# x + alpha * fx, streamed through one core: the stores on a queue of their own, with a small store of zeros ahead of them

## The chip, the cores and the metric

The kernel runs on one core of a Trainium2 chip. The metric is device time in microseconds, and lower is better. Three runs of the kernel before took 151.98 to 152.3 us, with a median of 152.07 us.

## The reference

The inputs are `x` and `fx`, both bfloat16 of 512 x 32 x 640, and one bfloat16 number `alpha`. The output has the shape and type of `x`.

```python
def reference(x, fx, alpha):
    return x + alpha * fx
```

Every element is read once from each of two arrays of 20.97 MB and written once to a third. That makes 62.92 MB through the DMA engines, and a multiply and an add for each element.

## The kernel before

The three arrays are seen as 128 partitions by 81920 elements, cut into 80 columns of K = 1024 elements (2 KB in each partition, 256 KB in all). A partition's whole row is contiguous in memory. `X` cuts `x` and the output into three pieces of 32, 32 and 16 columns. `FX` cuts `fx` into five of 16, 16, 19, 16 and 13. So the cuts of the two arrays are different, and a piece of `x` is finished by more than one piece of `fx`. `X_CUTS` loads the first 4 columns of piece 0 of `x` with a transfer of their own.

There are two buffers for pieces of `x` (pool `wide`) and two for pieces of `fx` (pool `fs`). The sum is made in place, in the buffer of `x`, and the store goes out of that buffer. A third piece of `x` must therefore wait until the store of the first has landed, and a third piece of `fx` until VectorE has used the first.

The order is written out by hand. `PLAN` is a list of steps that are emitted one after the other, and each engine and queue keeps that order for its own instructions:

- `x i` is `load_x` (L77): a load of piece i of `x`, issued on the sync queue (SP).
- `f j` is `load_f` (L85): a load of piece j of `fx`, issued on the sync queue.
- `c j i` is `compute` (L92): one VectorE instruction, `x_piece = fx_piece * alpha + x_piece`, over the columns that pieces j and i have in common.
- `s i` is `store` (L104): a store of piece i, issued on the sync queue.
- `a` is `alpha_to_lanes` (L111 to L117): alpha is loaded, and a matmul with a row of ones brings it to all 128 partitions.

```python
PLAN = "x 0, a, f 0, f 1, x 1, c 0 0, f 2, c 1 0, s 0, f 3, x 2, c 2 1, f 4, c 3 1, c 3 2, s 1, c 4 2, s 2"
```

(In the kernel there is one step on each line.) An instruction at the head of the sync queue that waits for a semaphore holds up all that stands behind it. With all loads and stores on that queue, the transfers also run in the order of the plan. ScalarE has no work in this kernel, and GpSimd (Pool) has four small memsets that the framework puts at the start.

`done` collects the instructions that a final no-op of the sync queue (`rest`, L126) waits for, all but the last store. After it comes the end of the program, which waits for everything.

Of the kernel before, what the change touches and what calls it, by code (L numbers as in the profile page):

```python
# [2 lines left out]

# [4 lines left out]

ACT = mybir.ActivationFunctionType
ALU = mybir.AluOpType  # L10
F32 = mybir.dt.float32
BF16 = mybir.dt.bfloat16

K = 1024
P = 128


X = [(0, 32), (32, 64), (64, 80)]
FX = [(0, 16), (16, 32), (32, 51), (51, 67), (67, 80)]

X_CUTS = {0: (4,)}
PLAN = """
x 0
a
f 0
f 1
x 1
c 0 0
f 2
c 1 0  # L30
s 0
f 3
x 2
c 2 1
f 4
c 3 1
c 3 2
s 1
c 4 2
s 2  # L40
"""


@with_exitstack
def kernel(
    ctx: ExitStack,
    tc: tile.TileContext,
    x: bass.AP,
    fx: bass.AP,
    alpha: bass.AP,  # L50
    out: bass.AP,
):

    nc = tc.nc
    xv = x.flatten_outer_dims().rearrange("(p n) d -> p (n d)", p=P)
    fxv = fx.flatten_outer_dims().rearrange("(p n) d -> p (n d)", p=P)  # L60
    ov = out.flatten_outer_dims().rearrange("(p n) d -> p (n d)", p=P)
    assert xv.shape[1] == X[-1][1] * K == FX[-1][1] * K

    consts = ctx.enter_context(tc.tile_pool(name="consts", bufs=1))
    psum = ctx.enter_context(tc.tile_pool(name="psum", bufs=1, space=bass.MemoryType.PSUM))
    wide = ctx.enter_context(tc.tile_pool(name="wide", bufs=2))
    fs = ctx.enter_context(tc.tile_pool(name="fs", bufs=2))
    ctx.enter_context(tc.manual_schedule())

    xt, ft = {}, {}  # L70
    done = []

    def load_x(i):
        a, b = X[i]
        xt[i] = wide.tile([P, max(e - s for s, e in X) * K], x.dtype, tag="x", name="x_t")
        for c, d in pairwise((a, *X_CUTS.get(i, ()), b)):
            r = nc.sync.dma_start(  # L77
                out=xt[i][:, (c - a) * K : (d - a) * K], in_=xv[:, c * K : d * K]
            )
            done.append(r)  # L80

    def load_f(j):
        a, b = FX[j]
        ft[j] = fs.tile([P, max(e - s for s, e in FX) * K], fx.dtype, tag="f", name="f_t")
        r = nc.sync.dma_start(out=ft[j][:, : (b - a) * K], in_=fxv[:, a * K : b * K])  # L85
        done.append(r)

    def compute(j, i):
        (fa, fb), (xa, xb) = FX[j], X[i]
        a, b = max(fa, xa), min(fb, xb)  # L90
        piece = xt[i][:, (a - xa) * K : (b - xa) * K]
        r = nc.vector.scalar_tensor_tensor(  # L92
            out=piece,
            in0=ft[j][:, (a - fa) * K : (b - fa) * K],
            scalar=lanes["a_f"][:],
            in1=piece,
            op0=ALU.mult,
            op1=ALU.add,
        )
        done.append(r)  # L100

    def store(i):
        a, b = X[i]
        r = nc.sync.dma_start(out=ov[:, a * K : b * K], in_=xt[i][:, : (b - a) * K])  # L104
        done.append(r)

    lanes = {}

    def alpha_to_lanes():
        a_1 = consts.tile([1, 1], alpha.dtype, name="a_1")  # L110
        done.append(nc.sync.dma_start(out=a_1[:], in_=alpha[None, :]))  # L111
        ones = consts.tile([1, P], alpha.dtype, name="ones")
        nc.vector.memset(ones[:], 1.0)  # L113
        a_ps = psum.tile([P, 1], F32, name="a_ps")
        done.append(nc.tensor.matmul(a_ps[:], ones[:], a_1[:], start=True, stop=True))  # L115
        lanes["a_f"] = consts.tile([P, 1], F32, name="a_f")
        nc.vector.tensor_copy(out=lanes["a_f"][:], in_=a_ps[:])  # L117

    does = {"x": load_x, "f": load_f, "c": compute, "s": store, "a": alpha_to_lanes}
    for step in PLAN.split("\n"):  # L120
        if step:
            what, *of = step.split()
            does[what](*map(int, of))


    rest = nc.sync.nop(nofuse=True)  # L126
    info = mybir.DependencyInfo(mybir.DependencyClass.Sync, mybir.DependencyReason.DATA)
    for i in done[:-1]:
        tc.add_manual_dep(rest.ins, i.ins.name, info, reason="all but the last store")


# [1 line left out]
_INS = ['x', 'fx', 'alpha']  # L133
_OUTS = [((512, 32, 640), 'bfloat16')]


# [23 lines left out]
```

## Time and profile before

| | us |
|---|---|
| median of three runs | 152.07 |
| span of the profiled execution | 150.2 |
| VectorE (DVE) busy | 86.8 |
| of that, the six steps of L92 | 86.5 |
| VectorE idle ahead of L92, waiting for a load of fx | 25.5 |
| sync queue waiting at L104 for VectorE | 56.2 |
| sync queue at L77 waiting for a store to land | 25.7 |

The profile gives no separate total for the profiled execution beside its span, so its span is compared with the median of the runs: that is 1.9 us above. In the profile, `SPq` is the sync queue as an issuer of transfers; "us to landing" is the time from the issue of a transfer to the arrival of its last part. A line of the timeline gives the start, the duration, the engine, the line of the kernel and the operation, and in square brackets how long the engine had been idle and what released it. DMA shares are means over the 16 DMA engines.

### The profile page before, as it was taken

How to read it: one execution, taken by the hardware profiler on the slowest of the kernel's cores; microseconds unless marked ns; L12 is line 12 of the kernel's file. 1: busy time of each engine (PE TensorE's matmuls, PEld its weight loads, DVE VectorE, ACT ScalarE, POOL GpSimd, SP SyncE). 2: the span in 40 equal slices, each digit the busy share in tenths (PEclk: the TensorE clock that was granted, in tenths of full speed). 3: DMA queues.
4: the chain of work that ended last, by engine and by line, in shares of the span. 5: the costliest groups of instructions: out<-in, count | busy, mean ns of one | idle time of the engine just before them, and what ended most of it. 6: DMA issues, size and time to landing. Idle time of an engine off the chain costs nothing.

```text
span 150.2 us, 78 instructions
## 1 busy us (share of the span) xinstructions
PE 0.2 (0%) x1; PEld 0.1 (0%) x1; DVE 86.8 (58%) x8; POOL 0.2 (0%) x4
## 2 busy tenths in 40 slices
PE   0000000000000000000000000000000000000000
PEld 0000000000000000000000000000000000000000
DVE  0000000049999999970399999106999999980000
POOL 0000000000000000000000000000000000000000
DMA  5997989999969696999696999999999969696994
GB/s 179 589 428 305 489 384 419 436 454 471 576 297 559 279 559 279 497 394 435 279 559 279 559 401 410 445 419 419 419 393 454 620 279 559 279 559 297 454 463 183
DMA packets 1730, 62.92 MB, mean 419 GB/s; under 512 B 194, under 2 KB 194, under 8 KB 194
## 3 DMA queue, kind: packets, MB, share of 16 engines
q1 hardware_dynamic: 1730, 62.92, 98.1%
HBM read 41.94 MB, written 20.97 MB: 419 GB/s over the span
## 4 chain that ended last, share of the span: by engine, by line
DMA 54%; DVE 35%; SPq 1%; issue 0%; DVEq 0%
DMA f_t<-in_fx_dram 54%; DVE x_t L92 35%; SPq L77 1%; SPq L111 0%; DVEq L92 0%
## 5 line engine op out<-in xcount | busy, mean ns | idle before, releaser
L92 DVE SCALAR_TENSOR_TENSOR x_t<-f_t,a_f,x_t 128x16384 bf16<-128x16384 bf16 (+3 forms) x6 | 86.5, 14438 | 25.5 <-DMA f_t<-in_fx_dram 25.5
L117 DVE COPY a_f<-a_ps 128x1 f32<-128x1 f32 x1 | 0.2, 159 | 21.5 <-PE a_ps L115 21.5
L113 DVE MEMSET ones<- 1x128 bf16 x1 | 0.2, 165 | 0.8 <-PEq L144 0.8
L115 PE MATMUL a_ps<-a,ones 1*128 1x1 bf16 x1 | 0.2, 158 | 22.2 <-DMA a<-in_alpha_dram 22.2
L144 POOL MEMSET const-bfloat16-1.0<- 128x1 bf16 x1 | 0.1, 103 | 0.0
L144 POOL MEMSET const-uint8-127<- 128x1 uint8 x1 | 0.1, 103 | 0.0
L115 PEld LDWEIGHTS <-ones 1*128 1x128 bf16 x1 | 0.1, 100 | 1.0 <-DVE ones L113 1.0
L144 POOL MEMSET const-float32-1.0<- 128x1 f32 x1 | 0.1, 100 | 0.0
L144 POOL MEMSET const-float32-0.0<- 128x1 f32 x1 | 0.1, 99 | 0.2 <-issue 0.2
## 6 DMA issues: line engine op xcount, KB each, us to landing
f_t<-in_fx_dram SPq DMA_DIRECT2D x3, 4096.0 KB, 35.6
x_t<-in_x_dram SPq DMA_DIRECT2D x1, 7168.0 KB, 21.3
f_t<-in_fx_dram SPq DMA_DIRECT2D x1, 4864.0 KB, 24.1
x_t<-in_x_dram SPq DMA_DIRECT2D x1, 4096.0 KB, 19.2
out_dram<-x_t SPq DMA_DIRECT2D x1, 4096.0 KB, 14.9
f_t<-in_fx_dram SPq DMA_DIRECT2D x1, 3328.0 KB
x_t<-in_x_dram SPq DMA_DIRECT2D x1, 1024.0 KB, 4.8
out_dram<-x_t SPq DMA_DIRECT2D x2, 24.7
```

The source lines that it names most:

```text
L77: r = nc.sync.dma_start(out=xt[i][:, (c - a) * K : (d - a) * K], in_=xv[:, c * K : d * K])
L92: r = nc.vector.scalar_tensor_tensor(out=piece, in0=ft[j][:, (a - fa) * K : (b - fa) * K], scalar=lanes["a_f"][:], in1=piece, op0=ALU.mult ...
L113: nc.vector.memset(ones[:], 1.0)
L115: done.append(nc.tensor.matmul(a_ps[:], ones[:], a_1[:], start=True, stop=True))
L117: nc.vector.tensor_copy(out=lanes["a_f"][:], in_=a_ps[:])
L144: nc = _bacc.Bacc("TRN2", target_bir_lowering=False, num_devices=1)
```

## The change

A tile of 128 x 256 zeros, `blank`, is made by a memset on GpSimd and stored to the first 256 elements of every row of the output. That store is issued on ScalarE's queue, as the first instruction of the kernel there. The later store of piece 0 writes the same places with the result, and it waits until the store of zeros has landed. All three stores of results are issued on ScalarE's queue too, in the same order. The sync queue keeps the loads of `x`, `fx` and alpha.

```diff
+HEAD = 256
 X_CUTS = {0: (4,)}
@@
     ctx.enter_context(tc.manual_schedule())
+    done = []
+
+    blank = consts.tile([P, HEAD], out.dtype, name="blank")
+    nc.gpsimd.memset(blank[:], 0.0)
+    done.append(nc.scalar.dma_start(out=ov[:, :HEAD], in_=blank[:]))
 
     xt, ft = {}, {}
-    done = []
@@
     def store(i):
         a, b = X[i]
-        r = nc.sync.dma_start(out=ov[:, a * K : b * K], in_=xt[i][:, : (b - a) * K])
+        r = nc.scalar.dma_start(out=ov[:, a * K : b * K], in_=xt[i][:, : (b - a) * K])
         done.append(r)
```

## The prediction

> **What bounds the kernel now.** I read the engine shares, then the DMA part, then the chain and the waits of the sync queue, and last the order of time around the three stores.
>
> ```profile
> span 150.2 us, 78 instructions
> PE 0.2 (0%) x1; PEld 0.1 (0%) x1; DVE 86.8 (58%) x8; POOL 0.2 (0%) x4
> DMA packets 1730, 62.92 MB, mean 419 GB/s; under 512 B 194, under 2 KB 194, under 8 KB 194
> q1 hardware_dynamic: 1730, 62.92, 98.1%
> ```
>
> VectorE is busy for 58%, the 16 DMA engines for 98.1%, all on one queue. 1730 less 194 small packets is 1536, or twelve transfers of 128: each partition row of a transfer is one packet, and each of the 16 engines carries 8 rows of every transfer. So the bound is bytes through the DMA engines, and the chain (54% DMA, 35% VectorE) only follows who released whom beside a full queue.
>
> ```profile
> out_dram<-x_t SPq DMA_DIRECT2D x1, 4096.0 KB, 14.9
> ...
> x_t<-in_x_dram SPq DMA_DIRECT2D x1, 1024.0 KB, 4.8
> ...
> x_t<-in_x_dram SPq DMA_DIRECT2D x1, 58.3
> ```
> ```profile
> 2.90 0.45 SPq L77 DMA_DIRECT2D x_t<-in_x_dram  x1
> ...
> 49.59 0.33 SPq L85 DMA_DIRECT2D f_t<-in_fx_dram  x1
> 66.78 0.35 SPq L104 DMA_DIRECT2D out_dram<-x_t  x1
> 67.19 0.42 SPq L85 DMA_DIRECT2D f_t<-in_fx_dram  x1
> 73.80 20.48 DVE L92 SCALAR_TENSOR_TENSOR x_t<-f_t,a_f,x_t 128x19456 bf16<-128x19456 bf16 x1 [7.04 <-DMA f_t<-in_fx_dram]
> 93.37 0.33 SPq L77 DMA_DIRECT2D x_t<-in_x_dram  x1
> 94.31 0.33 SPq L85 DMA_DIRECT2D f_t<-in_fx_dram  x1
> 102.84 17.41 DVE L92 SCALAR_TENSOR_TENSOR x_t<-f_t,a_f,x_t 128x13312 bf16<-128x13312 bf16 x2 [8.55 <-DMA f_t<-in_fx_dram]
> 116.95 17.96 SPq L104 DMA_DIRECT2D out_dram<-x_t  x2
> 120.46 14.08 DVE L92 SCALAR_TENSOR_TENSOR x_t<-f_t,a_f,x_t 128x13312 bf16<-128x13312 bf16 x1 [0.21 <-DMA f_t<-in_fx_dram]
> ```
>
> From these the landings: x 1 at 2.90 + 58.3 = 61.2; f 2 at 73.7 (VectorE starts on it); store 0 at 93.4 (x 2, which takes its buffer, is issued); f 3 at 102.8; f 4 at 120.4; the last store (the second in the merged line at 116.95, issued at 116.95 + 17.96 - 0.34 = 134.6, with 14.9 to landing) at 149.5; 0.7 of ending follows. Store 0 moves 32 columns of 1024 in 93.4 - 73.7 = 19.7; x 2 and f 4 move 29 in 17.6. That is 0.605 us a column for loads and stores alike. Two places stand out. f 2 has 19 columns, 11.5 us, and took 12.5: **1.0 us is lost**, just while the first store stands behind it in the queue. The second store, issued at 116.95 behind f 4, cost nothing: f 4 still landed on time. At the head, x 0's first 1 MB needs 2.4 us of data and lands 4.8 after issue. The busy times by window show no DMA (last two columns) until 1.7:
>
> ```profile
> 0.00:1.70 1.70, 0.00 (x0) 0.10 (x1) 0.17 (x1) 0.20 (x4) 1.00 0.00 0
> 1.70:5.50 3.80, 0.00 (x0) 0.00 (x0) 0.00 (x0) 0.00 (x0) 1.00 1.34 517
> ```
>
> So of the 4.8, about 1.0 is from issue (0.73) to first packet, 2.4 is data, and some 1.4 is a slow start.
>
> **The change part by part.** The sum is made against the span of 150.2; the median of 152.07 is 1.9 above it, and I keep that 1.9.
>
> *Issues.* Three store issues of 0.35 us leave the sync queue and four come to ScalarE's queue, which holds nothing else. In the compiled order f 3 now waits for VectorE's second step itself (it takes f 1's buffer), so it goes out at about 66.8 instead of 67.2. x 2 still waits for store 0 to land, f 4 for VectorE's third step behind it; stores 1 and 2 wait on ScalarE for their VectorE steps, with nothing queued behind them but each other. The DMA queue was full throughout: worth 0. The cover is f 2's or f 3's data still moving; if that runs out, an issue shows its 1.0.
>
> The Trainium skill (DMA: Bandwidth & Descriptors, "Issuing engines are not separate DMA queues") says that issuing from more engines saves only the sequencer's issue time. By that rule alone the sum would be 152.07 plus the blank's bytes, 152.2; the trace agrees about the issues but shows the 1.0 us at the first store, which the rule has no word for.
>
> *The blank store.* A Pool memset of 128x256 lies between 0.1 (Pool's 128x1 row) and perhaps 0.5 us, and only ScalarE's queue waits for it. 64 KB is a quarter of a column, 0.15 us of data. It has no row of its own: from 0.15, up to 1.2 if the first-store loss simply comes along to the head. Below 0.15 nothing can take it, as the bytes do move.
>
> *The loss at the first store.* It belongs to the first write only (the second had none). Between -1.0 (gone) and 0 (paid at the head instead). The blank's rows reach the engines at about 2.1 (Pool 0.75 to 1.0, issue, 1.0 latency), in the 1.4 us of slow start, so I take that most of it is covered: 0.3 paid. With the bytes: -1.0 + 0.3 + 0.15 = -0.55.
>
> *Sharing between the queues.* Before, a store waited its turn behind the loads. Now it shares each engine with them. No row of before has two queues, so this has bounds only. I take turns by packet, since a packet is a row here: a 64 KB row of store 0 (2.42 us) against a row of f 2 (1.44) or f 3 (1.21). At 67.8 f 2 has two or three rows left per engine; each waits for a store row, so f 2 lands at about 78 to 80. VectorE's third step (20.5) ends at 98.5 to 101. Store 0 lands at about 97.5, with three or four f 3 rows (3.6 us or more) left to hide x 2's 1.0. f 3 lands at 102 either way, as the bytes are the same. VectorE starts on f 3 there, store 1 goes out 14.1 later at 116.2, first packet 117.2; f 4 has two rows left (undisturbed it would land at 119.5), which wait for one or two store rows: 122.0 to 124.4. VectorE's last step ends at 136.1 to 138.5, store 2's first packet is at 137.1 to 139.5, and store 1 ends at 138.8. So a hole of **0 to 0.9 us** before the last store; half a microsecond of later start on ScalarE's queue, or a load row going first, closes it. I take 0, the end that two things lead to, and keep 0.9 in the range.
>
> The Trainium skill (same page, "Queues, rings and completion order") states that an engine goes round its queues and switches at packet boundaries. No row of before can confirm it. Were all 8 rows of a transfer one turn, store 0 would follow f 2 as before, and the sum would also be -0.55.
>
> Sum: 150.2 - 0.55 = 149.65 of span, 151.5 us.
>
> **The rivals.**
>
> *Even.* The loss is paid in full at the head (+0.15 of bytes), or the hole of 0.9 eats what is gained: -0.55 + 0.9 = +0.35 at most, 0 to +0.3 typically: 151.8 to 152.4. For it speaks that an engine that stalls on its first write stalls at the head too, with loads waiting.
>
> *Slower, loads and stores share by bytes.* If both queues get half of each engine whatever the row's size, the smaller f 3 overtakes store 0. f 2's 4.7 us left at 67.8 take 9.4, f 3's 9.7 take 19.4: it lands at 97. Store 0 then has some 5 left and lands at 102. Only then is x 2 issued, to an empty queue: 1.0 idle. VectorE has run ahead (third step to 98.3, fourth to 112.4), so store 1's packets start at 113.4 with nearly all of f 4 (7.9) still to come. At half speed f 4 lands at 128, VectorE's last step ends at 142, store 2's first packet is at 143, where store 1 ended at 140.2: 3 us idle. End 153.0 + 0.7 = 153.75: **+3.5, 155.6 us**, and up to +5.7 if the first-store loss stays as well. It decides as soon as f 3 lands before store 0. Against it: rows are the packets, and a store row is twice a load row.
>
> *Slower, mixing costs.* If each turn between a load row and a store row costs 0.1 us (nearest row: the 1.0 us that the two last f 2 rows of each engine lost, 0.5 a row), the some 20 turns of store 0 and store 1 cost 2.0, and the first-store loss is all that pays for it: with the hole, +0.5 to +2.5, 152.5 to 154.6. Against it: the handovers from store 0 to f 3 and from f 4 to store 1 show no loss.
>
> **How the numbers follow.** Forecast 0.41 (151.0 to 151.75); even 0.19, of which 0.17 is inside 0.2% (0.3 us, about what a measurement of this kernel can tell from no change) and 0.02 above; mixing or a kept loss with a hole 0.18; sharing by bytes 0.20; something not named here, on the slow side, 0.02. Faster 0.41, same 0.17, slower 0.42; the forecast is the likeliest single case, with 150.9 to 151.8 as its own range. The range reaches from 151.0 (the whole loss gone, blank free: 152.07 - 1.0) to 156.2, which takes in mixing and most of sharing by bytes.
>
> **What the changed profile would show.** f 2's landing, now 73.7, at 77 to 80 says that store 0 takes turns with it. The issue of x 2 before f 3's landing says turns by row; after it, sharing by bytes. VectorE's wait for f 4 grows from 0.2 us to some 2 to 5 in the forecast, to over 10 in the rival. The last store's issue against 134.6, and DMA idle ahead of it, gives the hole. x 0's first landing, 4.8 before, shows what the blank costs; store 0 to store 1 shows whether the rate stays at 0.605 a column. A ScalarE queue that is slow to start its first transfer, or a hole where both queues wait on each other's landing, would make the prediction wrong.

## The result

The changed kernel takes 155.66 us (four runs, 155.15 to 156.6) against 152.08 us: 1.024 times as long, with a 95% interval of 1.0221 to 1.0261. The profiled execution of it took 155.5 us around a span of 153.7, so the 1.8 us around the span are nearly the 1.9 of before. The loss of 3.5 us lies inside.

The head of the page, with the two DMA queues (packets, MB, share of the 16 engines):

```profile
span 153.7 us, 84 instructions
DMA packets 1874, 62.98 MB, mean 410 GB/s; under 512 B 210, under 2 KB 338, under 8 KB 338
q1 hardware_dynamic: 1298, 41.94, 65.4%
q10 hardware_dynamic: 576, 21.04, 31.7%
```

Loads and stores are now on two queues, and the shares add to 97.1% of a longer span. The bytes are the same but for the 64 KB of zeros. So either rows take longer or engines stand idle. The order of time around the stores says where (start, duration, engine, line, operation, idle time before it):

```profile
66.93 0.33 SPq L90 DMA_DIRECT2D f_t<-in_fx_dram  x1
66.93 73.88 ACTq L109 DMA_DIRECT2D out_dram<-x_t  x3
78.73 20.48 DVE L97 SCALAR_TENSOR_TENSOR x_t<-f_t,a_f,x_t 128x19456 bf16<-128x19456 bf16 x1 [11.83 <-DMA f_t<-in_fx_dram]
102.68 0.33 SPq L82 DMA_DIRECT2D x_t<-in_x_dram  x1
103.11 0.37 SPq L90 DMA_DIRECT2D f_t<-in_fx_dram  x1
103.80 17.41 DVE L97 SCALAR_TENSOR_TENSOR x_t<-f_t,a_f,x_t 128x13312 bf16<-128x13312 bf16 x2 [4.59 <-DMA f_t<-in_fx_dram]
126.35 14.08 DVE L97 SCALAR_TENSOR_TENSOR x_t<-f_t,a_f,x_t 128x13312 bf16<-128x13312 bf16 x1 [5.14 <-DMA f_t<-in_fx_dram]
```

Four things are to be read here. f 2 lands at 78.7 instead of 73.7, because store 0 now moves beside it. Store 0 lands only at 102.6, when x 2 is issued (93.4 before). f 3 lands at 103.8, 1.0 later than before. And f 4 lands at 126.3, 5.9 later than before, although the two loads x 2 and f 4 need only 17.6 us of data after f 3.

From the landings, stage by stage against the profile before (each is when the last of 16 engines finished):

| stage | before | after | longer by |
|---|---|---|---|
| to x 1 | 61.24 | 61.37 | 0.13 |
| f 2, store 0, f 3 | 41.58 | 42.40 | 0.8 |
| x 2 | 9.71 | 11.15 | 1.45 |
| f 4 and store 1 | 27.27 | 28.31 | 1.0 |
| store 2 | 9.65 | 9.66 | 0 |
| ending | 0.74 | 0.83 | 0.1 |

The stage of x 2 holds a hole. The windows show it; their last two columns are the DMA share (a packet counts where it starts) and GB/s:

```profile
99.00:101.00 2.00, 0.00 (x0) 0.00 (x0) 0.21 (x1) 0.00 (x0) 1.00 0.84 360
101.00:103.00 2.00, 0.00 (x0) 0.00 (x0) 0.00 (x0) 0.00 (x0) 1.00 0.38 164
103.00:105.00 2.00, 0.00 (x0) 0.00 (x0) 1.20 (x1) 0.00 (x0) 1.00 0.91 262
```

The packet records explain it. They do not name the engine, but the rows of one engine can be told apart, since each starts as the one before it ends. On 14 of the 16 engines store 0's first row starts between 71.5 and 72.1 and from there store rows and load rows take turns, one each; these engines land their parts of store 0 at 99.9 to 100.4 and are through with f 3's data at 102.0 to 102.5. On two engines the first store row starts at 74.1 and 74.3, and some of their store rows take 2.45 to 2.65 us instead of 2.42. They land store 0 at 102.5 and 102.6. x 2 may overwrite store 0's buffer only when the last engine has landed its part, so 14 engines run dry and wait for two, and then 1.0 more for the first row of x 2. That first row is slow as well (1.3 to 2.2 us instead of 1.21).

One more thing holds up the landings. Each engine ends its part of a transfer with a record of 4 bytes. In the kernel before, store 0's starts as its last row ends (92.3 to 92.7 on the 16 engines). With two queues it takes a turn of its own. The last rows of store 0 end at 98.35 to 98.9 on the 14 engines and at 101.0 and 101.1 on the two; the 4 bytes start at 99.6 to 100.1 and at 102.2 and 102.3, a row of f 3 (1.2 us) later. So it is in all seven kernels here that issue store 0 on ScalarE's queue at 67. f 2's 4 bytes in turn stand behind a whole row of store 0: on the 14 engines its data end at 75.4 to 75.9, and the 4 bytes start at 77.8 to 78.3. As an estimate from these numbers, a store 0 that landed 1.2 us earlier would have brought x 2's first row at about 102.4, where the 14 engines end f 3, with hardly a hole.

The stage of f 4 and store 1 shows no idle engine. There the last two load rows of f 4 on each engine are stretched, from 0.99 to about 1.6 us each, ahead of store 1's first row.

### The profile page after: what moved, and what is told of

The parts are those of the page before. It is cut to its first block, busy times and chain, and to the rows that moved or that the text cites. A ratio compares the mean times of both kernels' runs of the same rounds, so it can differ in the third digit from the quotient of the medians.

```text
span 153.7 us, 84 instructions
## 1 busy us (share of the span) xinstructions
PE 0.2 (0%) x1; PEld 0.1 (0%) x1; DVE 86.8 (56%) x8; POOL 0.5 (0%) x5
## 4 chain that ended last, share of the span: by engine, by line
DMA 58%; DVE 32%; SPq 1%; issue 0%; DVEq 0%
DMA f_t<-in_fx_dram 35%; DVE x_t L97 32%; DMA out_dram<-x_t 23%; SPq L82 1%; SPq L116 0%; DVEq L97 0%; SPq L90 0%
```

## The experiments

The records give one more number for each run, which the table and the text below call stretch: the time by which load rows took longer than the usual for their size, as a mean over the 16 engines.

**Which part of the change costs.** Four kernels undo it part by part.

The changed kernel without the zeros:

```diff
-    blank = consts.tile([P, HEAD], out.dtype, name="blank")
-    nc.gpsimd.memset(blank[:], 0.0)
-    done.append(nc.scalar.dma_start(out=ov[:, :HEAD], in_=blank[:]))
```

> The stores stay on ScalarE's queue and the store of zeros is left out. Theory 1 (the loss at the start of a store beside loads has nothing to do with a first write, so the zeros buy nothing): 0.15 us less than the changed kernel, about 155.5 us, span 153.5, with f 2's last rows still slowed. Rival (the zeros do shelter store 0's start on the new queue): store 0's first row comes at least 1 us later than its 4.6 after issue, and the time is 156.5 us or more.

The zeros alone, all three stores on the sync queue:

```diff
-        r = nc.scalar.dma_start(out=ov[:, a * K : b * K], in_=xt[i][:, : (b - a) * K])
+        r = nc.sync.dma_start(out=ov[:, a * K : b * K], in_=xt[i][:, : (b - a) * K])
```

> The store of zeros stays on ScalarE's queue, the three stores go back to the sync queue. Theory 1 (the loss at f 2 is not of the first write): f 2 lands 12.5 us after x 1 as before, time 152.2 us (before plus 0.15). Rival (it is the first write of the kernel, and the changed kernel's loss is another one): f 2 lands 11.5 after x 1, time 151.2 us.

Store 0 back on the sync queue, stores 1 and 2 on ScalarE's (with the zeros):

```diff
-        r = nc.scalar.dma_start(out=ov[:, a * K : b * K], in_=xt[i][:, : (b - a) * K])
+        r = (nc.sync if i == 0 else nc.scalar).dma_start(out=ov[:, a * K : b * K], in_=xt[i][:, : (b - a) * K])
```

> Store 0 is back on the sync queue behind f 2, stores 1 and 2 stay on ScalarE's. Theory 1 (about 1 us lost where a store starts on a queue that has been empty, plus a hole at x 2): the hole of 1.5 us at x 2 is gone, the loss of about 1.0 at store 1 stays: span about 151.4, 153.3 us. Rival (loads and stores sharing the engines is what costs, in proportion to the time they share): store 1 shares for only some 5 us of the 40 in all, so nearly everything is won back: 152.3 us.

The reverse, only store 0 on ScalarE's queue (with the zeros):

```diff
-        r = nc.scalar.dma_start(out=ov[:, a * K : b * K], in_=xt[i][:, : (b - a) * K])
+        r = (nc.scalar if i == 0 else nc.sync).dma_start(out=ov[:, a * K : b * K], in_=xt[i][:, : (b - a) * K])
```

> Only store 0 is on ScalarE's queue, stores 1 and 2 are back on the sync queue. Theory 1: the hole at x 2 of about 1.5 us and the two late engines (0.8) stay, the 1.0 at store 1 is gone, f 4's rows run at full speed: span 152.7, 154.5 us. Rival (the second loss comes of the program being late or of the stores' place, not of a queue that starts): f 4's last rows are slowed in this kernel too, 155.5 us.

| kernel | us | ratio to before | stretch at f 2 | stretch at f 4 |
|---|---|---|---|---|
| without the zeros | 154.57 | 1.0166 [1.0149, 1.0183] | 1.2 | 1.2 |
| zeros alone | 152.06 | 1.0003 [0.9994, 1.0013] | 0.75 | 0.05 |
| store 0 on sync | 152.06 | 1.0006 [0.9996, 1.0015] | 0.8 | 0.04 |
| store 0 alone on ScalarE | 155.85 | 1.0252 [1.023, 1.0274] | 0.9 | 1.3 |

(Before: 1.3 at f 2 and 0.04 at f 4; the changed kernel: 1.2 and 1.2.)

The whole loss comes of store 0. With it back on the sync queue nothing is left, although stores 1 and 2 stay on ScalarE's; with it alone on ScalarE's all of it is there. My "theory 1" missed with the third kernel: a store that starts on an empty queue loses nothing (0.04 at f 4). It missed with the fourth too, where store 1 is on the sync queue and f 4's rows are stretched all the same. So the second loss belongs neither to a queue nor to its start. The rival named with the third kernel, that sharing the engines is itself the cost, fits these four; what speaks against it comes below, with the hole filled and the zeros left out.

The zeros do not remove the stretch at f 2: 0.75 with them lies within the 0.7 to 1.3 that it has over the kernels here without them, and the time shows nothing won. But where store 0 is on ScalarE's queue they cost 1.1 us, where 0.15 was expected. That was tried again, below.

In the third kernel x 2 goes out at 93.55 with all of f 3 still to move, and the window that held the hole is full:

```profile
93.55 0.33 SPq L82 DMA_DIRECT2D x_t<-in_x_dram  x1
94.71 0.33 SPq L90 DMA_DIRECT2D f_t<-in_fx_dram  x1
103.25 17.41 DVE L97 SCALAR_TENSOR_TENSOR x_t<-f_t,a_f,x_t 128x13312 bf16<-128x13312 bf16 x2 [8.57 <-DMA f_t<-in_fx_dram]
117.37 17.96 ACTq L109 DMA_DIRECT2D out_dram<-x_t  x2
120.88 14.09 DVE L97 SCALAR_TENSOR_TENSOR x_t<-f_t,a_f,x_t 128x13312 bf16<-128x13312 bf16 x1 [0.21 <-DMA f_t<-in_fx_dram]
```
```profile
101.00:103.00 2.00, 0.00 (x0) 0.00 (x0) 0.00 (x0) 0.00 (x0) 1.00 0.84 360
```

Here store 1 is issued on ScalarE's queue while f 4 still has 3.5 us to go, and VectorE waits 0.21 us for f 4, as in the kernel before.

**The hole.** The first attempt to close it cut piece 0 of x into two tiles with a store each, so that x 2 (there the piece x 3) waits for half a store. It was done to the changed kernel and, as a control, to the kernel before.

```diff
-X = [(0, 32), (32, 64), (64, 80)]
+X = [(0, 16), (16, 32), (32, 64), (64, 80)]
...
+    half = ctx.enter_context(tc.tile_pool(name="half", bufs=2))
...
-        xt[i] = wide.tile([P, max(e - s for s, e in X) * K], x.dtype, tag="x", name="x_t")
+        xt[i] = (wide if i == 2 else half).tile([P, (b - a) * K], x.dtype, tag="x", name="x_t")
```

(and the plan with one more load and one more store.)

> The changed kernel with piece 0 of x cut into two tiles of 16 columns, stored one after the other on ScalarE's queue, so that the load that was x 2 needs only the first half's store to have landed. Theory 2 (the loss is the hole that opens because that load waits for the last of the 16 engines to finish store 0, and the hole in turn brings the second loss, f 4's slow rows ahead of store 1): the load goes out near 90, no hole, f 4's rows at full speed; what stays is the 0.15 for the zeros and up to 0.8 at f 2: 152.1 to 153.0 us. Rival (two queues taking turns is itself the cost): 154.5 us or more.

> The kernel before with the same two tiles of 16 columns and the same two half stores, all on the sync queue. Theory 2: there is no hole to be closed and the transfers keep their order, so it is the time of before, 152.0 us, within 0.3. Rival (the cut by itself is worth time): 151.5 us or less, and then the run of the changed kernel with halves must be read against this one.

They took 155.7 us (1.0249 [1.0229, 1.0269]) and 151.94 us (0.9997 [0.9989, 1.0006]). The control is as expected, the other is a miss, and by my own edit: with a tile of its own, the first half needs only VectorE's first step, so ScalarE's queue issued its store at 50.0 instead of 67.

```profile
79.12 0.33 SPq L85 DMA_DIRECT2D x_t<-in_x_dram  x1
88.00 51.80 DVE L100 SCALAR_TENSOR_TENSOR x_t<-f_t,a_f,x_t 128x19456 bf16<-128x19456 bf16 x4 [20.84 <-DMA f_t<-in_fx_dram]
108.51 0.33 SPq L93 DMA_DIRECT2D f_t<-in_fx_dram  x1
```

The load goes out at 79.1 and the hole at 102 is gone, but the early store took turns with x 1 and f 2. f 2 landed at 88.0, VectorE ended its fourth step at 122.5, and store 1 waited for that while the loads were through at 120.4: by the records 3.7 us of idle engines, at 119.6 to 123.3. It is the same loss at another place: a store that goes ahead of loads delays the work that the next store needs. The time is where the rival had put it (154.5 or more), but as a test of the hole it settled nothing.

The second attempt leaves the tiles alone and exchanges two steps of the plan. At 99.2 VectorE has freed f 4's buffer, but f 4 stood behind x 2 on the sync queue, which was waiting for store 0.

```diff
 f 3
-x 2
 c 2 1
 f 4
+x 2
 c 3 1
```

> The changed kernel with two steps of the plan exchanged: the load f 4, whose buffer is free at 99.2, goes out ahead of the load x 2, which waits until store 0 has landed at 102.6. Theory 2 (the loss is the hole at 102 to 104, and the slow rows ahead of store 1 are its consequence): f 4's data fill the hole and no load row is slowed ahead of store 1; of the 3.5 us some 2.5 come back, 153.0 us. Theory 2b (the hole costs 1.5, the slow rows ahead of store 1 have another cause and stay): 154.1 us. Rival (taking turns itself is the cost, and the hole only a sign of it): 155.0 us or more.

And the control, the same exchange in the kernel before:

> The kernel before with the same exchange of f 4 and x 2, all on the sync queue: the control. Theory 2: there is no hole to fill, 152.0 us; up to 152.6 if the later landing of x 2 holds up VectorE's last step and with it store 2 (the last step would end at 138.0, store 1 at 139.8). Rival (the order of the two loads is worth time by itself): 151.4 us or less.

The two took 153.44 us (1.0094 [1.0078, 1.0111]) and 152.03 us (1.0005 [0.9995, 1.0014]). The issues of the first (the x2 are f 3 at 67.05 and f 4 at 99.1; then x 2), and its window, as above:

```profile
67.05 32.40 SPq L90 DMA_DIRECT2D f_t<-in_fx_dram  x2
103.14 0.33 SPq L82 DMA_DIRECT2D x_t<-in_x_dram  x1
```
```profile
101.00:103.00 2.00, 0.00 (x0) 0.00 (x0) 0.00 (x0) 0.00 (x0) 1.00 0.86 371
```

The hole is filled, and the stretch of load rows ahead of store 1 is gone with it (0.03 instead of 1.2). On ten engines store 1's own first row took 3.1 to 3.5 us instead of 2.42, but not on the two engines that landed it last. On the same chip the changed kernel took 155.83, so this one exchange wins 2.4 us of 3.9, where the stage table says 1.45 + 1.0. The time is 0.4 us above theory 2's forecast and 0.7 below that of 2b. Theory 2, that the second loss is a consequence of the hole, stands this test.

**The zeros.** The changed kernel and the one without the zeros were run once more, beside each other on one chip.

> The changed kernel unchanged, beside the next run on one chip. Both theories: 155.2 to 155.9 us.

> The changed kernel without the store of zeros, beside the run before it on one chip. If the zeros cost what their bytes and their place at the head cost, it is 0.15 to 0.35 us under the run before, 155.3 us. If the 1.0 us by which the first such run was faster belongs to the zeros, 154.6 us.

155.83 us (1.0257 [1.024, 1.0274]) and 154.67 us (1.0189 [1.0162, 1.0216]). The 1.1 us is there again. Then both undone edits together, the exchange and no zeros:

> The changed kernel with f 4 ahead of x 2 and without the store of zeros. If the zeros cost 1.1 us and the hole with its successor 2.4, independently, 152.3 us, 0.3 above before. If the zeros cost only through the hole (they leave a few engines later, and x 2 waits for the latest), they cost no more than their 0.2 to 0.4 at the head where the hole is filled: 153.1 us.

152.14 us, 1.0014 [1.0004, 1.0025]: level with before to within a quarter of a per cent, although all three stores are on ScalarE's queue. So the two are independent and add up: 2.4 for the hole with its successor, 1.2 for the zeros, 0.2 left. That the zeros cost through the hole falls, and so does the rival that sharing the engines is itself the cost: store 0 shares them here as it did.

Of the 1.2, some 0.3 us is lost at the head (x 0's second part landed at 22.58 to 23.04 in six profiles with the zeros, at 22.45 to 22.62 in eight without). The rest is in the stage of f 2, store 0 and f 3, which lasted 42.86 us in the exchanged kernel with the zeros and 41.53 without. There the engines split into those on which store 0's first row starts at 71.1 to 72.2 and those on which it starts a load row or so later, at 72.8 to 74.4. In the four profiles with the zeros and store 0 (whole) on ScalarE's queue the late ones were the few, 2, 5, 2 and 7, and it was their store rows that were stretched, the longest to 2.65, 3.05, 2.66 and 2.97 us. Without the zeros 8, 9 and 13 were late, and few rows of theirs were stretched; in the last of these it was the three early engines whose rows were, and they were not the last to land. That is what the records show; why 64 KB stored at 5 us should change the split at 72 us, no run here shows.

**What stretches load rows ahead of a store.** I supposed ("theory 3") that it is the time that a store waits behind moving loads: 5.9 us at f 2, 3.5 at f 4 in the kernel before. One kernel makes the wait longer, the other shorter, both with all stores on the sync queue.

```diff
-FX = [(0, 16), (16, 32), (32, 51), (51, 67), (67, 80)]
+FX = [(0, 16), (16, 32), (32, 51), (51, 64), (64, 80)]
```

> The kernel before with fx cut at 64 instead of 67, so that VectorE's fourth step is three columns shorter and store 1 is issued some 2.7 us earlier while f 4 ends at the same time; nothing else moves, all on one queue. Theory 3 (a store that is issued more than about 4 us ahead of the end of the loads it stands behind slows their last rows by about 1.0 us in all, as at f 2; at 3.5 us it does not, as at f 4 before): f 4's last rows grow and the time is 153.0 us. Rival (the loss at f 2 belongs to store 0 alone, and the second loss of the changed kernel to its queue): 152.0 us.

```diff
-X = [(0, 32), (32, 64), (64, 80)]
-FX = [(0, 16), (16, 32), (32, 51), (51, 67), (67, 80)]
+X = [(0, 32), (32, 63), (63, 80)]
+FX = [(0, 16), (16, 32), (32, 46), (46, 63), (63, 80)]
+LAST = {2: (73,)}
```

(`LAST` cuts the last VectorE step and the last store in two.)

> The kernel before with x cut at 32 and 63 and fx at 16, 32, 46 and 63, so that f 2 has 14 columns and ends 2.3 us after store 0 is issued instead of 5.9; the last VectorE step and the last store are cut in two, as the last piece is longer. Theory 3: f 2's last rows are not slowed, 1.0 us less than before, 151.0 us. Rival (the loss comes with the first store wherever it stands): 152.0 us.

152.17 us (1.0012 [1.0, 1.0025]) with a stretch of 0.26 at f 4, and 152.73 us (1.0045 [1.003, 1.0061]). The second did lose its stretch at f 2 (0.05), and gave more than that back at once: store 0's last rows and the first of f 3 were slow, f 3 landing 11.56 us after store 0 where its 17 columns need 10.3. The first does not fit theory 3. The second fits it at f 2 alone, and its time missed both forecasts. A last run lets store 1 wait far longer on the one queue of the kernel before; it leaves out five columns of VectorE's fourth step:

```diff
+        if (j, i) == (3, 1):
+            b -= 5
...
 c 3 1
-c 3 2
 s 1
+c 3 2
```

> The kernel before with VectorE's fourth step five columns shorter (those five columns of the output stay x, so part of the computation is left out) and store 1 issued right behind it, at about 111.5, some 9 us ahead of the end of f 4, all on the sync queue. Theory 3 (a store that stands for more than some 5 us behind moving loads slows their last rows, by about 1 us): f 4's last rows grow as they do at f 2, 153.0 us. Rival (the slow rows belong to store 0, and to a start behind a hole): 152.0 us.

151.99 us (1.0007 [0.9998, 1.0017]), stretch 0.09, with store 1 issued at 111.6 and f 4 landing at 120.4:

```profile
102.81 8.75 DVE L94 SCALAR_TENSOR_TENSOR x_t<-f_t,a_f,x_t 128x8192 bf16<-128x8192 bf16 x1 [8.53 <-DMA f_t<-in_fx_dram]
111.59 23.29 SPq L106 DMA_DIRECT2D out_dram<-x_t  x2
112.57 3.42 DVE L94 SCALAR_TENSOR_TENSOR x_t<-f_t,a_f,x_t 128x3072 bf16<-128x3072 bf16 x1 [1.01 <-DMA x_t<-in_x_dram]
120.43 14.08 DVE L94 SCALAR_TENSOR_TENSOR x_t<-f_t,a_f,x_t 128x13312 bf16<-128x13312 bf16 x1 [4.43 <-DMA f_t<-in_fx_dram]
```

Theory 3 falls. Over all profiles the stretch ahead of store 1 is 1.1 to 1.3 us in the five with a hole at x 2 and under 0.3 in the others. The stretch goes with a late start of the store: store 1's first row came 4.8 to 5.0 us after its issue in the four of those five that have it on ScalarE's queue, and 1.0 to 2.3 us in the three kernels that have it there, beside moving loads, and no hole. What in a hole brings this about some 17 us later stays open, and so does the stretch at f 2.

## Why the prediction was wrong

The forecast was 151.5 us, faster. By its own steps:

- *Bytes bound it, and the issues are worth nothing.* Right. With two steps exchanged and no zeros, all stores on ScalarE's queue cost 0.2 us.
- *Turns by packet, a row each.* Right: the records show store row, load row, store row. The numbers that fit do so in part by luck. f 2 landed at 78.7, forecast 78 to 80 from two or three rows that each wait for a store row; on 14 engines it was one row and then the 4 bytes, for which the sum had no term. VectorE's wait for f 4 was 5.14 us, forecast some 2 to 5, but from turns with store 1 that did not happen. x 2 was issued (102.68) ahead of f 3's landing (103.8), the sign that was named for turns by row, but 14 engines had ended f 3 by then.
- *"Store 0 lands at about 97.5, with three or four f 3 rows (3.6 us or more) left to hide x 2's 1.0."* This step failed, and it carries the 2.4 us of the hole and its successor. It landed at 102.6. First, I took 1.0 us from issue to first packet from a load at the head; store 0 needed 4.6 (66.93 to 71.5). Fewer rows of f 2 were left to go between its rows, so that on 14 engines its last row still ended at 98.35 to 98.9. Secondly, I took the end of the data for the landing: the turn of the 4 bytes put 1.2 us on it, and some 0.3 passed from there to the landing. Thirdly, I reckoned one engine and took it for all. 14 engines did have their three rows of f 3 left at the end of store 0, but a landing is the last engine's, and two were 2 to 2.7 us behind. The hole was 1.45 us with its slow restart, and it drew 1.0 more at f 4, for which the sum had no term.
- *The hole before the last store, 0 to 0.9.* There was none (and by the times given there, 139.5 against 138.8, its upper end is 0.7): store 2 was issued at 140.5, store 1 ended at 143.2. f 4's rows did not take turns with store 1 as supposed, since its first row came only after all of them (117.9 to 122.9).
- *The loss at the first store, -1.0 + 0.3.* Wrong in its cause. It was read as the first write's, because the second store showed none. With a write ahead of it the stretch at f 2 is still 0.75 to 1.2, and it turned up at store 1 too. Nothing of it was won in time.
- *The zeros, 0.15 to 1.2.* The upper bound held (1.2 with the exchange, 1.1 without), but I took 0.45, and most of the price was not at the head, where I looked for it.

The rival "loads and stores share by bytes" gave 155.6 us and a span of 153.75, and the measured ones are 155.66 and 153.7. That is a coincidence. It asked for f 3 ahead of store 0, for f 4 at half speed beside store 1, and for 3 us of idle time ahead of store 2; none of the three happened. What it had right is the kind of loss, x 2 issued to queues that had run dry, which it priced at 1.0. The Trainium skill's rule of turns at packet boundaries (DMA: Bandwidth & Descriptors, "Queues, rings and completion order") is what the records show, with a row of 32 to 64 KB as the packet. Its rule that issuing from more engines saves only issue time ("Issuing engines are not separate DMA queues") says nothing of a loss; the change lost 3.6 us, of which the exchange of two loads wins 2.4.

## What to carry to other kernels

When the DMA queue is full, its order is the schedule: a store moved to a queue of its own is moved ahead of loads, and what must be asked is which load then waits for whom. A landing is the slowest of 16 engines, and its last record takes a turn like a row, so a load that waits for a store needs cover for the spread of the engines (here 2.7 us) and for one row of the other queue (here 1.2), and not only for the issue; a step of the plan that is already free, put ahead of the waiting one, gives that cover for nothing. And a rival that hits the time is not yet the cause: compare its signs too.

## What the runs showed of the hardware

- A store's first row beside moving loads on the other queue came 1.0 to 5.0 us after its issue: 4.0 to 4.6 for store 0 in all seven kernels that issue it there at 67, and the load rows ahead of it then took 0.7 to 1.2 us longer in all, as a mean over the engines; the 512-byte rows of the zeros came after 3.6 to 3.8 us. A load at the head needs 1.0.
- With two queues, an engine gives a row to each in turn whatever the rows' sizes, 64 KB against 32 KB. The 4 bytes that end an engine's part of a transfer take such a turn too: store 0's came 1.2 us, a load row, after its data, and where f 2 ended, its 4 bytes stood between two store rows, so that the store got two rows in a row.
- An engine that falls behind stays behind, since each engine has its fixed 8 rows of every transfer. With store 0 on ScalarE's queue its landings spread over 1.3 to 3.4 us in the seven kernels, against 0.35 us in the kernel before and at most 0.7 in the others with store 0 whole on the sync queue.
- After a hole the first load row is slow: 1.8 us instead of 1.21, as a mean over the engines of the changed kernel.
- No version that was tried is clearly faster than the kernel before.
